# Later chunks copy x ahead of routing, and weight fetches move with seven raw buffers

## The chip, the cores and the metric

One core of a Trainium2 chip runs the kernel. The metric is device time in microseconds (us); lower is better. The engines are TensorE (PE in the rows, its weight loads PEld), VectorE (DVE), ScalarE (ACT), GpSimd (POOL) and SyncE (SP), which issues most DMAs. Each engine works through its own instructions in program order.

## The reference

Two stages follow each other: a linear attention with a decaying state (batch 4, 8 heads, 768 steps, head size 48), and a mixture of 8 experts with one expert per token (top 1) over its 3072 output rows.

```python
for t in range(S):
    cur = einsum('bhd,bhe->bhde', u[None] * k_t, v_t)
    y_t = einsum('bhd,bhde->bhe', r_t, state + cur)
    state = w[None, :, :, None] * state + einsum('bhd,bhe->bhde', k_t, v_t)
x = y.transpose(0, 2, 1, 3).reshape(3072, 384)
logits = x @ w_gate                      # 8 experts
expert = argmax(logits); gate = softmax(logits)[expert]
# each expert takes its tokens in order, up to a capacity of 768
out[i] = gate[i] * (relu(x[i] @ w1[expert]) @ w2[expert])
```

## The kernel before

**Attention.** The 3072 rows are worked on in NI = 24 chunks of 128, one turn of the loop `for i in range(NI)` each. PE makes score products (`scores`, L448), the value and state products (`values` L484, `inter` L493) and the state update (L459). DVE applies the mask (`masks`, L451) and copies the chunk's result out of PSUM (`turn`, L497, tile `yt`). In the next turn PE transposes that copy (`flip`, L504) and makes the router's logits from it (`logits`, L511). Two or three products without use (`fresh`, L524) stand ahead of `flip`. ACT copies the transposed rows (`rows`, L515) and SP stores them in the DRAM tensor `x_dr` (L519).

**Routing.** When the logits of a group of chunks are there, a generator `route` does that group in stages: `choose` on DVE (L76 to L111, ending with `lane`), rank products on PE (L114 to L117), slots and gate values on DVE (L121 to L158), a product on PE that turns them into table entries (L169), and the addition to the table on DVE (L171). `advance("t")` runs the next stage that waits for PE, `advance("v")` the next of DVE. The group of chunks 18 to 20 goes through `choose` in turn 21, its slots in turn 22 and its table product in turn 23. The group of chunks 21 to 23 comes after the loop. When chunks 0 to 17 are in the table, `ide` (L173) names the first 256 rows of expert 0 and POOL gathers them; `ids` (L175) names all the rest after the last group, and POOL then issues one gather per tile of rows (`gather`, L249, tile `xg`).

**After the loop.** PE transposes the 256 gathered rows (L263); ACT and DVE split them in two parts `xh` and `xl` (L267, L268), so that each fp32 product is made of three. The *early* part multiplies them with the first weights of expert 0 (`early`, L301 to L303, tile `e`), with the last stages of routing between its eight steps. Six products without use (`warm`, L547) follow, then PE transposes the two other tiles of expert 0 (L263) and makes their first layer (`layer1`, L280 to L282). From there PE runs layer 1 and layer 2 (L319 to L321) of the eight experts.

**Weights.** SP fetches raw weights into a pool `wrw` with `bufs=4` (`fetch`, L224, or in two halves L664 in the loop); ACT and DVE split each raw buffer into two parts `ws` (`split`, L234 and L235). A raw buffer is free for the next fetch when its two splits are done. `PLAN0` says in which turn a fetch or a split of expert 0 stands; `next(ws)` does its next entry. In turn 22 it splits entries 6 and 7, in turn 23 entry 8, entries 9 to 13 stand in the early part. `w1s` is the same for expert 1; it starts after the loop, with two of its three first fetches in the early part.

Of the kernel before, what the change touches and what calls it, by code (L numbers as in the profile page):

```python
# [19 lines left out]
NI = B * NC  # L20
# [6 lines left out]
PLAN = [((0, 1, 2), ())] + [((n // 2 + 3,) if n % 2 == 0 and n < 8 else (), (n,)) for n in range(14)]  # L27
# [7 lines left out]
def rwkv_moe(nc, tc, dmj, rkv, bdc, wp, wv, uv, wgp, wg, w1, w2, out, cap):  # L35
# [3 lines left out]
    with ExitStack() as ctx:  # L39
# [57 lines left out]
        def advance(slot, most=1 << 30):  # L97
            for r in list(routing):
                if r[1] == slot and most:
                    most -= 1  # L100
                    r[1] = next(r[0], None)
                    if r[1] is None:
                        routing.remove(r)
# [93 lines left out]

        with ExitStack() as mc:
            wsp = [mc.enter_context(tc.tile_pool(name="wsp", bufs=1))]
            wrw = mc.enter_context(tc.tile_pool(name="wrw", bufs=4))  # L200
            keep = mc.enter_context(tc.tile_pool(name="keep", bufs=1))
            sm = mc.enter_context(tc.tile_pool(name="sm", bufs=2))
            ps1 = mc.enter_context(tc.tile_pool(name="ps1", bufs=1, space=PSUM))
# [8 lines left out]
            def wset(e):  # L212
                wtiles[e] = [wsp[e % 2].tile([128, 3 if i < 2 else 8, F if i < 2 else DM], F32R,
                                             tag=f"ws{i}", name=f"ws{i}_{e}") for i in range(4)]
                return wtiles[e]

            def wstream(e, plan, later=None):
                raw = {}

                def fetch(k):  # L220
                    r = raw[k] = wrw.tile([128, F if k < 3 else 2 * DM], F32, tag="wr", name=f"wr{k}_{e}")
                    src = w1[e, :, k] if k < 3 else w2[e, :, 2 * k - 6:2 * k - 4].rearrange("p f d -> p (f d)")
                    if later is None:
                        nc.sync.dma_start(out=r, in_=src)  # L224
                    else:
                        later.extend([(r[64 * h:64 * h + 64], src[64 * h:64 * h + 64]) for h in range(2)])

                def split(n):
                    k, j = divmod(n, 2)
                    m, i, o = (0, k, 512) if k < 3 else (2, n - 6, DM)  # L230
                    c = slice(o * j, o * j + o) if k < 3 else slice(0, DM)
                    hi, lo = (wtiles[e][m + t][:, i, c] for t in range(2))
                    r = raw[k][:, o * j:o * j + o]
                    nc.scalar.copy(out=hi, in_=r)  # L234
                    nc.vector.tensor_tensor(out=lo, in0=r, in1=hi.bitcast(F32), op=ALU.subtract)  # L235

                for fetches, splits in plan:
                    if splits and e not in wtiles:
                        wset(e)
                    for k in fetches:  # L240
                        fetch(k)
                    for n in splits:
                        split(n)
                    yield
# [242 lines left out]
            def inter(i):  # L487
                t = T[i]
                if t["s0"] is None:
                    return  # L490
                for p in range(NP):
                    for a in range(2):
                        nc.tensor.matmul(yrows(p, a), lhsT=t["s0"][row(a), p], rhs=t["rt"][row(a), p], start=False, stop=p >= 2)  # L493

            def turn(i):
                yt = T[i]["yt"] = wk.tile([PR, 2, 256], F32, tag="yt", name=f"yt{i}")
                nc.vector.tensor_copy(out=yt, in_=py[0:PR, :, 0:256])  # L497
# [39 lines left out]
            def each(f, i, *more):  # L537
                if i < NI:
                    f(i, *more)
# [124 lines left out]
                    nc.sync.dma_start(out=r, in_=src)  # L664

            ws = wstream(0, PLAN0, parts)
            more = setup3()
            for i in range(NI):
                if i >= 2:
                    store(i - 2, nc.sync)  # L670
                part()
                each(product, i + 3)
                each(diag, i + 2, range(0, 2))
                each(scores, i + 1)
                if i == 0:
                    warm(2)
                else:
                    fresh(i - 1, 2)
                    flip(i - 1)
                    rows(i - 1)  # L680
                advance("t")
                each(update, i + 1)
                if i >= 1:
                    logits(i - 1)
                    if i + 3 >= NI:
                        keep_turn(i - 1)
                each(diag, i + 2, range(2, NP))
                if i == NI - 2:
                    gather(0, ide, (0, 1), C * SNAP)
                each(masks, i + 1)  # L690
                each(prep_k, i + 3)
                each(carry, i + 1)
                each(prep_state, i + 3)
                each(load, i + 7, 1)
                each(load, i + 7, 2)
                part()
                if i >= NI - 2:
                    next(ws)
                if i == NI - 1:
                    store(i - 1, nc.sync)  # L700
                advance("v")
                values(i)
                each(load, i + 6, 3)
                if i == 0:
                    bonus_alone(3)
                elif i + 3 < NI:
                    bonus(i + 3, lg[:, E:])
                if 0 < i < NI - 3:
                    keep_turn(i - 1)
                inter(i)  # L710
                turn(i)
                each(prep_r, i + 3)
                each(load, i + 7, 0)
                if i >= 1:
                    next(more, None)
                if i < NI - 2:
                    next(ws)
            while parts:
                part()
            w1s = wstream(1, [((k,), ()) for k in range(3)] + PLAN[1:])  # L720
            next(w1s)
            lc.close()
            buf = mc.enter_context(tc.tile_pool(name="act", bufs=1, side="right"))
            hh, hl = (buf.tile([128, 8, W1S], F32R, name=n) for n in ("hh", "hl"))
# [9 lines left out]
            keep_turn(NI - 1, lo)  # L734
            rows(NI - 1)
            store(NI - 1, nc.sync)
            for s_ in [xtrans(0, j, (0, 1)) for j in range(3)]:
                s_()
            advance("v")
            for f in range(8):  # L740
                if f % 2 == 0:
                    product_, split_ = early(f // 2)
                product_(f % 2)
                if f in (0, 2, 5):
                    advance("t")
                    advance("v")
                if f == 2:
                    gather(0, ids[:, 0:4], (2, 3))
                    gather_all(1)
                if f % 2:  # L750
                    split_()
                if f > 2:
                    next(ws, None)
                if f in (3, 5):
                    next(w1s)
            assert not routing
            warm(6)
            ac.close()
# [5 lines left out]
            ws = w1s  # L764
# [4 lines left out]
            for k in range(E):  # L769
# [10 lines left out]
                if k + 1 < E:  # L780
# [5 lines left out]
                    if k + 2 < E:  # L786
                        ws = wstream(k + 2, PLAN)
# [246 lines left out]
```

## Time and profile before

| what | value |
|---|---|
| median of 3 runs | 410.23 us (409.98 to 411.45) |
| profiled execution | 410.22 us |
| its span, first to last instruction | 408.4 us |
| PE busy | 386.5 us, 95% of the span |
| PEld busy | 349.0 us, 85% |
| DVE busy | 242.8 us, 59% |
| ACT busy | 190.1 us, 47% |
| POOL busy | 139.9 us, 34% |
| moved by DMA | 59.23 MB, 145 GB/s over the span |

The shares are means over stages with different limits, so the stage is looked at by itself. The chain that ended last is 58% PE, 21% issue, 8% DVE, 5% DMA and 5% POOL. About 1.8 us of the profiled execution lie outside its span.

### The profile page before, as it was taken

To read this page: it belongs to the slowest core of one execution; us is meant where nothing else is said; L and a number is where in the kernel's file an instruction comes from. 1 tells how busy PE (TensorE), PEld (TensorE's weight loads), DVE (VectorE), ACT (ScalarE), POOL (GpSimd) and SP (SyncE) were. 2 spreads that over 40 slices of the span, in tenths; PEclk is the share of its full clock that TensorE was granted. 3 is DMA by queue.
4 is the path that set the end of the run, shared out by engine and by line. 5 is a ranking of instruction groups with operands and counts; after the bars stand their busy time and mean duration, and the time that the engine had idled before them with its cause. 6 is when DMAs were issued, how large, how long until landed. Compare 5 with 4: busy or idle time off the path is not lost.

```text
span 408.4 us, 10083 instructions
## 1 busy us (share of the span) xinstructions
PE 386.5 (95%) x3883; PEld 349.0 (85%) x3884; DVE 242.8 (59%) x546; ACT 190.1 (47%) x496; POOL 139.9 (34%) x198
## 2 busy tenths in 40 slices
PE   8999999999999685999999999999999999999993
PEld 4588888888877574999999999999999999999992
DVE  6587989999998564654644635635635535534310
ACT  3666666676654132532733733633633633622401
POOL 3677468478443016103303303303303300300203
PEclk9999999999999698899999999999999999999998
DMA  6786997977723306354444444444544533500102
GB/s 175 230 245 196 262 241 237 241 236 206 215 81 87 102 20 211 107 155 157 146 134 158 135 134 156 136 139 146 148 134 152 155 126 91 161 16 1 58 1 69
DMA packets 28714, 59.23 MB, mean 145 GB/s; under 512 B 5194, under 2 KB 14450, under 8 KB 28656
## 3 DMA queue, kind: packets, MB, share of 16 engines
q1 hardware_dynamic: 25072, 49.05, 41.7%
q0 software_dynamic: 3584, 9.44, 6.9%
q8 instruction: 32, 0.52, 0.6%
q14 instruction: 26, 0.21, 0.2%
HBM read 49.38 MB, written 9.78 MB: 145 GB/s over the span
## 4 chain that ended last, share of the span: by engine, by line
PE 58%; issue 21%; DVE 8%; DMA 5%; POOL 5%; another core or an unknown queue 1%; SPq 1%; POOLq 1%; ACT 0%; DVEq 0%
PE b L319 6%; PE a L280 5%; PE a L281 5%; PE a L282 5%; PE b L320 5%; PE b L321 5%; POOL out L328 4%; PE pk L448 3%; PE warm L547 3%; DMA dm<-dmj 3%; PE py L484 2%; PE tp L263 2%; DMA wr<-w 2%; PE py L493 2%; PE pu L411 2%
## 5 line engine op out<-in xcount | busy, mean ns | idle before, releaser
L235 DVE TENSOR_TENSOR ws<-wr,ws 128x384 fp32r<-128x384 f32 (+1 forms) x112 | 66.7, 613 | 5.1 <-ACT ws L234 4.4
L328 POOL DMA_INDIRECT out<-yo,ids x32 | 31.2, 976 | 108.9 <-ACT yo L327 102.1
L280 PE MATMUL a<-xh,ws 128*128 128x412 f32 (+1 forms) x192 | 68.3, 356 | 0.0
L319 PE MATMUL b<-hh,ws 128*128 128x412 f32 (+1 forms) x192 | 68.0, 354 | 0.0
L282 PE MATMUL a<-xh,ws 128*128 128x412 f32 (+1 forms) x192 | 66.0, 343 | 0.0
L281 PE MATMUL a<-xl,ws 128*128 128x412 f32 (+1 forms) x192 | 65.9, 343 | 0.0
L320 PE MATMUL b<-hl,ws 128*128 128x412 f32 (+1 forms) x192 | 65.7, 342 | 0.0
L321 PE MATMUL b<-hh,ws 128*128 128x412 f32 (+1 forms) x192 | 65.7, 342 | 0.0
L249 POOL DMA_INDIRECT xg<-x_dr,ids x30 | 30.2, 1006 | 101.8 <-PE tp L263 74.7
L285 ACT ACTIVATE hh<-a 128x412 fp32r<-128x412 f32 (+1 forms) x64 | 31.2, 488 | 71.9 <-PE a L282 71.9
L286 DVE SCALAR_TENSOR_TENSOR hl<-a,hh 128x412 fp32r<-128x412 f32 (+1 forms) x64 | 35.4, 553 | 45.2 <-ACT hh L285 43.4
L234 ACT CAST ws<-wr 128x384 fp32r<-128x384 f32 (+1 forms) x112 | 59.9, 557 | 0.0
L322 DVE COPY yt<-b 128x412 f32<-128x412 f32 (+1 forms) x24 | 13.7, 570 | 72.6 <-PE b L321 56.7
L424 ACT ACTIVATE s<-idn,lb 128x128 f32<-128x128 f32 x160 | 51.1, 392 | 0.5
L404 POOL TENSOR_TENSOR z<-dm 112x256 f32<-112x256 f32 x48 | 38.1, 813 | 7.4 <-DMA dm<-dmj 7.4
L267 ACT CAST xh<-tp 128x412 fp32r<-128x412 f32 (+2 forms) x27 | 12.4, 469 | 54.8 <-PE tp L263 52.9
L280 PEld LDWEIGHTS a<-xh,ws 128*128 128x128 f32 x192 | 36.8, 192 | 0.2
L319 PEld LDWEIGHTS b<-hh,ws 128*128 128x128 f32 x192 | 36.1, 188 | 0.9
L281 PEld LDWEIGHTS a<-xl,ws 128*128 128x128 f32 x192 | 36.8, 192 | 0.1
L282 PEld LDWEIGHTS a<-xh,ws 128*128 128x128 f32 x192 | 36.6, 191 | 0.1
L320 PEld LDWEIGHTS b<-hl,ws 128*128 128x128 f32 x192 | 36.2, 188 | 0.1
L321 PEld LDWEIGHTS b<-hh,ws 128*128 128x128 f32 x192 | 36.1, 188 | 0.2
(161 smaller groups left out, 624.2 us busy)
## 6 DMA issues: line engine op xcount, KB each, us to landing
wr<-w SPq DMA_DIRECT2D x21, 512.0 KB
wr<-w SPq DMA_DIRECT2D x28, 384.0 KB
dm<-dmj SPq DMA_DIRECT2D x88, 96.0 KB
bk<-bdc SPq DMA_DIRECT2D x24, 192.0 KB
bv<-bdc SPq DMA_DIRECT2D x24, 192.0 KB
x_dr<-x SPq DMA_DIRECT2D x24, 192.0 KB
wr<-w SPq DMA_DIRECT2D x6, 256.0 KB
wr<-w SPq DMA_DIRECT2D x8, 192.0 KB
```

Of the source, the lines that this page charges most:

```text
L234: nc.scalar.copy(out=hi, in_=r)
L235: nc.vector.tensor_tensor(out=lo, in0=r, in1=hi.bitcast(F32), op=ALU.subtract)
L280: nc.tensor.matmul(o, lhsT=wh, rhs=xh[:, d, a:z], start=d == 0, stop=False)
L281: nc.tensor.matmul(o, lhsT=wh, rhs=xl[:, d, a:z], start=False, stop=False)
L282: nc.tensor.matmul(o, lhsT=wl, rhs=xh[:, d, a:z], start=False, stop=d == 2)
L286: nc.vector.scalar_tensor_tensor(out=hl[:, f, b:z], in0=o[:, b - a:], scalar=0.0, in1=hh[:, f, b:z].bitcast(F32), op0=ALU.max, op1=ALU.sub ...
L319: nc.tensor.matmul(o, lhsT=wh, rhs=hh[:, f, :n], start=f == 0, stop=False)
L320: nc.tensor.matmul(o, lhsT=wh, rhs=hl[:, f, :n], start=False, stop=False)
L321: nc.tensor.matmul(o, lhsT=wl, rhs=hh[:, f, :n], start=False, stop=f == 7)
L328: r = nc.gpsimd.indirect_dma_start(out=out[:, :], out_offset=bass.IndirectOffsetOnAxis(ap=ids[:q, at:at + 1], axis=0), in_=yo, in_offset=N ...
L404: nc.gpsimd.tensor_tensor(out=z[:, p:p + 2], in0=t["dm"][:, 0, p:p + 2], in1=t["dm"][:, 1, p:p + 2], op=ALU.mult)
L424: nc.scalar.mul(out=s[:, a, p], in_=idn, mul=t["bon"][:, 2 * p + a:2 * p + a + 1])
```

## The change

In turns 21 to 23 `advance("t")` goes from ahead of `update` to behind `inter`, and `advance("v")` from ahead of `values` to behind `turn`. `next(ws)` is the last step of every turn now. The fetch plan of expert 1 is made ahead of the loop, and one of its three w1 fetches (512 KB) is issued at the end of each of turns 21, 22 and 23; the two fetches in the early part are gone. The pool `wrw` has 7 buffers. After the loop, `choose` of the last group stands ahead of the splits of the early rows, and the split of the first early tile is issued in step 2, behind the routing stage there, and not in step 1.

```diff
-            wrw = mc.enter_context(tc.tile_pool(name="wrw", bufs=4))
+            wrw = mc.enter_context(tc.tile_pool(name="wrw", bufs=7))
...
             ws = wstream(0, PLAN0, parts)
+            w1s = wstream(1, [((k,), ()) for k in range(3)] + PLAN[1:])
...
-                advance("t")
+                if i < NI - 3:
+                    advance("t")
                 each(update, i + 1)
...
                 part()
-                if i >= NI - 2:
-                    next(ws)
                 if i == NI - 1:
                     store(i - 1, nc.sync)
-                advance("v")
+                if i < NI - 3:
+                    advance("v")
                 values(i)
...
                 inter(i)
+                if i >= NI - 3:
+                    advance("t")
                 turn(i)
+                if i >= NI - 3:
+                    advance("v")
+                    next(w1s)
                 each(prep_r, i + 3)
                 each(load, i + 7, 0)
                 if i >= 1:
                     next(more, None)
-                if i < NI - 2:
-                    next(ws)
+                next(ws)
             while parts:
                 part()
-            w1s = wstream(1, [((k,), ()) for k in range(3)] + PLAN[1:])
-            next(w1s)
...
-            for s_ in [xtrans(0, j, (0, 1)) for j in range(3)]:
+            flipped = [xtrans(0, j, (0, 1)) for j in range(3)]
+            advance("v")
+            for s_ in flipped:
                 s_()
-            advance("v")
...
-                if f % 2:
+                if f == 2:
+                    early_()
+                if f == 1:
+                    early_ = split_
+                elif f % 2:
                     split_()
                 if f > 2:
                     next(ws, None)
-                if f in (3, 5):
-                    next(w1s)
```

The first place is DVE in turns 22 and 23. Before, `masks` (L451) is followed by two weight splits (L235), the slots and values of the routing group (L121 to L158), and only then the copy of chunk 22 (L497, `yt_2585`):

```order
L451 COPY_PREDICATED s_2426<-msk,pk 128x1024
L235 TENSOR_TENSOR ws_0_1137<-wr_0_1839,ws_0_1136 128x384 x2
L121 TENSOR_TENSOR pr<-pr,oh_2483 128x24
...
L158 TENSOR_TENSOR at_2564<-pr,lo_2555 128x384
L497 COPY yt_2585<-py 112x512
L235 TENSOR_TENSOR ws_0_1137<-wr_0_2120,ws_0_1136 128x384
L171 TENSOR_TENSOR tab<-tab,pr 128x96
L497 COPY yt_2629<-py 112x512
```

In the change, on the same engine at the same place (the copies of chunks 22 and 23 are `yt_2567` and `yt_2630`):

```order
L451 COPY_PREDICATED s_2426<-msk,pk 128x1024
L497 COPY yt_2567<-py 112x512
L121 TENSOR_TENSOR pr<-pr,oh_2501 128x24
...
L158 TENSOR_TENSOR at_2580<-pr,lo_2571 128x384
L235 TENSOR_TENSOR ws_0_1137<-wr_0_1839,ws_0_1136 128x384 x2
L497 COPY yt_2630<-py 112x512
L171 TENSOR_TENSOR tab<-tab,pr 128x96
L235 TENSOR_TENSOR ws_0_1137<-wr_0_2120,ws_0_1136 128x384
```

The copy of chunk 22 moved ahead of the routing and of the two splits; the copy of chunk 23 stands behind both. In turn 21 the copy likewise moved ahead of the table addition and `choose`, which stand ahead of L451 in both kernels.

The second place is DVE after the loop, where `xl` is the split of the early rows, `lane` the end of `choose` and `hl` the split of an early tile. Before:

```order
L268 TENSOR_TENSOR xl<-tp_2_0_2679,xh 128x256
L76 TENSOR_REDUCE pr<-lb 128x3
...
L111 TENSOR_TENSOR lane<-lane,pr 128x8
L121 TENSOR_TENSOR pr<-pr,oh_2693 128x24
...
L158 TENSOR_TENSOR at_2720<-pr,lo_2716 128x384
L308 SCALAR_TENSOR_TENSOR hl<-e_2699,hh 128x2x256
L171 TENSOR_TENSOR tab<-tab,t_2747 128x32
L175 TENSOR_SCALAR ids<-tab 128x32
```

In the change:

```order
L76 TENSOR_REDUCE pr<-lb 128x3
...
L111 TENSOR_TENSOR lane<-lane,pr 128x8
L268 TENSOR_TENSOR xl<-tp_0_0_2677,xh 128x256
...
L121 TENSOR_TENSOR pr<-pr,oh_2691 128x24
...
L158 TENSOR_TENSOR at_2724<-pr,lo_2720 128x384
L171 TENSOR_TENSOR tab<-tab,t_2749 128x32
L175 TENSOR_SCALAR ids<-tab 128x32
```

`choose` moved ahead of the three splits, and the first `hl` went behind `ids` and the gate values.

The third place is SP's queue from turn 21 to the first fetches of w2 (`wr_0` are buffers of expert 0, `wr_1` of expert 1; 128x1024 is a w1 fetch of 512 KB, 128x768 a w2 fetch of 384 KB). Before:

```order
L519 DMA x_dr<-x_2340 128x384
L519 DMA x_dr<-x_2446 128x384
L664 DMA wr_0_2507<-w 64x768 x2
L519 DMA x_dr<-x_2525 128x384
L519 DMA x_dr<-x_2595 128x384
L224 DMA wr_1_2631<-w 128x1024
L519 DMA x_dr<-x_2670 128x384
L224 DMA wr_1_2790<-w 128x1024
L224 DMA wr_1_2822<-w 128x1024
L224 DMA wr_1_2906<-w 128x768
```

In the change:

```order
L519 DMA x_dr<-x_2340 128x384
L224 DMA wr_1_2507<-w 128x1024
L519 DMA x_dr<-x_2446 128x384
L664 DMA wr_0_2509<-w 64x768 x2
L224 DMA wr_1_2585<-w 128x1024
L519 DMA x_dr<-x_2527 128x384
L519 DMA x_dr<-x_2599 128x384
L224 DMA wr_1_2633<-w 128x1024
L519 DMA x_dr<-x_2674 128x384
L224 DMA wr_1_2906<-w 128x768
```

The three w1 fetches stand among the stores of chunks 19 to 23, and the first w2 fetch comes directly behind the last store. The buffers that the second and third w1 fetch of before waited for (those of entries 9 and 11) are taken by the second and third w2 fetch in the change.

## Rows read from the trace of the kernel before

**Rows 1.** The page's 40 slices of the span (10.2 us each), in tenths, and GB/s.

```profile
PE   8999999999999685999999999999999999999993
PEclk9999999999999698899999999999999999999998
...
GB/s 175 230 245 196 262 241 237 241 236 206 215 81 87 102 20 211 107 155 157 146 134 158 135 134 156 136 139 146 148 134 152 155 126 91 161 16 1 58 1 69
```

**Rows 2.** Windows: start:end length, busy us per engine, granted clock, DMA share, GB/s.

```profile
165.00:401.00 236.00, 236.00 (x1353) 228.01 (x1352) 112.95 (x217) 100.50 (x214) 50.91 (x52) 1.00 0.39 118
```

**Rows 3.** PE's timeline, turn 21 to early part: start, us, what, [idle <-releaser].

```profile
125.91 0.40 PE L169 MATMUL pr<-val,at 128*128 128x96 f32 x2
126.24 0.56 PE L459 MATMUL pu<-bv,kt 128*48 128x48 f32 x16
...
128.08 0.66 PE L493 MATMUL py<-rt,st 48*48 48x128 f32 x16
...
130.65 0.60 PE L504 MATMUL xp<-idn,yt 112*128 112x112 f32 x4 [0.28 <-DVE yt L497]
...
132.75 0.65 PE L493 MATMUL py<-rt,st 48*48 48x128 f32 x16
...
137.18 1.01 PE L504 MATMUL xp<-idn,yt 112*128 112x112 f32 x4 [3.24 <-DVE yt L497]
...
143.61 0.64 PE L511 MATMUL lo<-wgt,yt 112*64 112x8 f32 x16
...
148.22 0.17 PE L114 MATMUL pr<-oh,tri 128*128 128x24 bf16 x1 [1.04 <-DVE lane L111]
```

**Rows 4.** DVE's timeline over the same stretch.

```profile
127.83 0.24 DVE L171 TENSOR_TENSOR tab<-tab,pr 128x96 f32<-128x96 f32 x1
...
129.91 0.68 DVE L497 COPY yt<-py 112x512 f32<-112x512 f32 x1
130.51 1.29 DVE L451 COPY_PREDICATED s<-msk,pk 128x1024 f32<-128x1024 int32 x1
132.62 1.03 DVE L235 TENSOR_TENSOR ws<-wr,ws 128x384 fp32r<-128x384 f32 x2 [0.81 <-ACT ws L234]
133.56 0.18 DVE L121 TENSOR_TENSOR pr<-pr,oh 128x24 f32<-128x24 f32 x1
...
135.98 0.55 DVE L158 TENSOR_TENSOR at<-pr,lo 128x384 fp32r<-128x384 int32 x1
...
145.61 1.08 DVE L268 TENSOR_TENSOR xl<-tp,xh 128x256 fp32r<-128x256 f32 x3 [2.35 <-ACT xh L267]
```

**Rows 5.** Windows with the granted clock (the number ahead of the DMA share).

```profile
137.20:143.40 6.20, 6.20 (x58) 4.67 (x58) 1.41 (x3) 1.05 (x3) 0.00 (x0) 0.50 0.36 119
164.00:167.00 3.00, 3.00 (x14) 2.72 (x15) 0.64 (x2) 0.72 (x3) 1.95 (x2) 0.50 0.41 144
167.30:172.00 4.70, 4.70 (x42) 4.70 (x41) 3.92 (x9) 3.46 (x9) 0.00 (x0) 1.00 0.24 64
```

**Rows 6.** PE's timeline from the end of the early part.

```profile
156.52 1.47 PE L547 MATMUL warm<-wz 128*128 128x512 bf16 x6
157.83 0.44 PE L263 MATMUL tp<-idn,xg 128*128 128x128 f32 x2
163.18 1.35 PE L263 MATMUL tp<-idn,xg 128*128 128x128 f32 x4 [4.91 <-remote]
```

**Rows 7.** Waits between 150 and 165 us: us in total, times, longest.

```profile
ACT hh L307 <- remote: 4.5, 1, 4.5
```

**Rows 8.** Windows of 2 us around that wait.

```profile
156.00:158.00 2.00, 2.00 (x13) 1.12 (x12) 1.20 (x3) 0.00 (x0) 1.70 (x2) 1.00 0.91 318
158.00:160.00 2.00, 0.27 (x2) 0.13 (x1) 0.00 (x0) 0.00 (x0) 1.39 (x3) 1.00 0.96 352
```

**Rows 9.** First gather by `ids` (POOL's timeline), three weight fetches (SP's, 150 to 165).

```profile
151.65 1.00 POOL L249 DMA_INDIRECT xg<-x_dr,ids  x1 [20.03 <-DVE pr L91]
...
153.94 8.51 SPq L224 DMA_DIRECT2D wr<-w  x3
```

## The prediction

> **What bounds the kernel now.** I read the page's slices first, to find where the end is decided. PE is full except in slices 14 to 16, which span 133 to 163 us, and the clock dips in the same place [rows 1]. From 165 to 401 us PE is busy in all 236 us at full clock [rows 2]: the experts start when the stage before lets them, and nothing behind it can absorb or return a gain. So the question is by how much the first layer of expert 0 starts earlier. Weight buffers and prefetch in the expert stage are hidden by PE itself.
>
> I then followed PE through that stage, asking of each idle time who ended it. In turn 23 PE waits 3.24 us for DVE's copy of chunk 22 [rows 3]. DVE had the chunk's result at 133.4, when `inter` (132.75, 0.65 long) ended, but had two weight splits and the slots of a routing group in its queue until 136.53 [rows 3, 4]. [...] A second idle time of 1.04 us comes at 148.22, where the rank product waits for `lane`, the end of `choose` [rows 3]. The third is the longest: after `warm` and two transposes PE stops for 4.91 us until 163.18, with no releaser that the profile knows [rows 6], and ACT waits 4.5 us in the same way for a tile whose products PE had long made [rows 7]. It falls in the only place where DMA moves 318 to 352 GB/s over 4 us, against a mean of 20 in the slice before [rows 1, 8]. After it the clock is at 0.50 once more until about 167.3 [rows 5].
>
> **The change, step by step.**
>
> *Turn 21.* The table product (two matmuls, 0.33 us from 125.91 to the next row at 126.24) goes behind `inter`, which ends at 128.4 in place of 128.74 [rows 3]. DVE copies chunk 21 at once (0.68 us, to 129.1), then does table addition and `choose` (127.83 to 129.91 before, 2.08 us) until 131.2 and `masks` (1.29 us) until 132.5 [rows 4]. `masks` ended at 131.8 before, so 0.7 us later; nothing asks for its result until `values` of turn 23. PE's wait of 0.28 us ahead of `flip` in turn 22 is gone [rows 3].
>
> *Turn 22.* `inter` ended at 133.40. It loses that 0.28 us and about 0.2 us of rank products that go behind it: 132.95. DVE is free at 132.5, copies chunk 22 until 133.65, and `flip` runs at 133.7 in place of 137.18. **That is 3.5 us.**
>
> *Turn 23.* From `flip` to the end of `inter` PE took 2.75 us in turn 22 at full clock (130.65 to 133.40) [rows 3], 2.55 without the rank products: 136.3. But DVE still has the slots and values (133.56 to 136.53, 2.97 us) and the two splits (1.03 us) ahead of the copy of chunk 23 [rows 4]: 133.65 + 2.97 + 1.03 = 137.65, and the copy ends at 138.3. DVE, not PE, decides here. `lo` starts at 138.4 and not at 143.61: **5.2 us in all**, the 3.5 us included. What is left of idle PE time is under 1 us in two pieces; 1.04 us did not bring the clock down at 148.22, so I leave it up. [...]
>
> *Early part.* `choose` takes 1.53 us (from the end of `xl` at 146.69 to the rank at 148.22) [rows 3, 4]. It moves into the time in which DVE waits 2.35 us for ACT's `xh` [rows 4], but starts only with the last logits, so about 0.5 us of it pushes `xl`. The 1.04 us wait becomes about 0.35 us ahead of the third product: **0.7 us**, between 0 and 1.04. The first `hl` behind `ids` costs nothing: layer 2 needs it only when all of layer 1 is done, and it lets `ids` and the gathers come 0.7 us earlier too, so the gathers keep their lead on PE.
>
> So far 5.2 + 0.7 = 5.9 us: 410.2 - 5.9 = 404.3 us. This rests on waits of engines for each other and is the firm part.
>
> *The stop at 158 us.* Here the trace gives a coincidence and no cause. Before, two w1 fetches of 512 KB are issued from 153.94 on, as splits free two buffers, on top of the gathers that began at 151.65 [rows 9]. In the change those w1 fetches are done by then. But the same two buffers are now wanted by w2 fetches, which SP holds ready, so the same two releases start 384 KB each. The burst gets thinner, 768 KB for 1024, and does not disappear. The first of its fetches also comes later against the gathers, since one `hl` (about 0.7 us) is now ahead of the split that frees the buffer. Bounds: nothing of the 4.91 us is left, or all of it. Before, 4.05 us lie from the first fetch (153.94) to the end of `warm` (157.99) [rows 6, 9]; now about 3.4. Scaling by bytes and by that time, 4.91 x 0.75 x 3.4 / 4.05 = 3.1 us are left, an estimate between the two ends; 1.8 us are won.
>
> *The clock behind it.* [...] It fell behind idle times of 3.24 and 4.91 us and not behind 1.04. With 3.1 us it could go either way; I let it stay up, since part of the old fall came in a stop half as long again: 2.05 us won. Sum: 5.9 + 1.8 + 2.05 = 9.75 us, so **400.5 us**, by the profiled execution's own 410.22, which is the median of the runs but for 0.01. The 1.8 us outside the span stay.
>
> *The rest.* Three more buffers, and the fetches moved up: SP issues them among the stores of chunks 19 to 23, and only the gathers by `ids` wait for the last of these stores. DMA moves 81 to 102 GB/s in the slices from 112 to 143 us, where the first eleven slices reach 262 [rows 1], so 512 KB per turn fits. Nothing, then, as long as that store lands before `ids` is there; each us beyond would delay the late gathers by as much.
>
> **The rivals.**
>
> *The stop goes wholly* (A): no burst is dense enough to hold PE. 4.91 + 2.05 more than the firm part: 397.3 us. For it: nowhere else in the trace does PE stop so, in slices of up to 262 GB/s [rows 1]. Against: the same two releases.
>
> *The stop stays whole* (C): 404.3 us. For it: its length isn't explained by bytes, since it lasted until 163.18, after the densest window [rows 8]. [...]
>
> *The stop moves up* (D), the case on the other side: in turn 22 one w1 fetch and 384 KB of expert 0 now meet the two gathers by `ide`. If PE's hand-over to a copy is held there as at 158 us, 4.9 + 2.05 us are added to 404.3: 411.3 us, slower than before. It decides from a hold of 5.9 us on. For it: the densest windows were reached with two fetches and gathers in flight [rows 8, 9], and here two fetches and two gathers meet. Against: gathers and a 384 KB fetch ran there before without it.
>
> *The copy stays behind DVE* (E): turn 23 gains only the 3.5 us, or the clock falls in it, and the stop is whole: 406 to 408 us.
>
> **How the numbers follow.** A 0.27, my forecast 0.37 (with the clock down it is 402.5), C 0.22, D 0.07, E 0.07. The range from 396.8 to 404.9 holds the first three and leaves out D, E and a little. About 0.5% (2 us) is what a measurement can tell here from no change. Faster by more: 0.91 (A, forecast, C, most of E). Within: 0.05. Slower: 0.04.
>
> **What would show it.** `flip` of turn 23 about 3.5 us after the one of turn 22 began and at full clock; L235 twice directly ahead of the copy of chunk 23; `lo` at 138 to 139; no wait ahead of L114; the first L280 near 153 if A holds, 156 if I am right, 158 to 160 if C. It is wrong if PE's clock is at 0.50 anywhere from 133 to 150, if the transposes of the late tiles wait for a gather by name, or if layer 1 of expert 0 has gaps, in which case w2 and w1 of the next experts have moved the burst under it.

## The result, and the profile after

The changed kernel takes 405.81 us (median of 4 runs, 404.90 to 406.39) beside 410.11 for the kernel before: a ratio of 0.9887, 95% interval [0.9858, 0.9916]. The gain is 4.3 us. The forecast was 9.7. Every ratio in this document is of fast runs alone, those within 1.5% of the fastest of their kernel. The profiled execution of the changed kernel takes 405.67 us with a span of 403.9.

The slices of its page (10.1 us each, in tenths, and GB/s), which answer to [rows 1]:

```profile
PE   8899999999989894999999999999999999999993
...
PEclk9999999999999997999999999999999999999999
...
GB/s 178 232 237 218 259 239 226 253 209 223 235 69 138 189 123 153 140 110 145 210 78 144 207 80 142 208 80 137 216 80 141 217 82 79 60 2 1 59 1 69
```

The hole of before in slices 14 and 15 is all but closed (8 and 9 now). One hole is left, slice 16 with its 4, and the clock dips in the same slice. PE's timeline from turn 22 to the early part, answering to [rows 3]:

```profile
130.12 0.55 PE L504 MATMUL xp<-idn,yt 112*128 112x112 f32 x4
...
133.79 0.60 PE L504 MATMUL xp<-idn,yt 112*128 112x112 f32 x4 [0.36 <-DVE yt L497]
...
136.74 0.54 PE L169 MATMUL pr<-val,at 128*128 128x96 f32 x3 [0.28 <-DVE at L158]
...
138.37 0.64 PE L511 MATMUL lo<-wgt,yt 112*64 112x8 f32 x16 [0.43 <-DVE yt L497]
...
141.25 0.39 PE L303 MATMUL e<-xl,ws 128*128 128x256 f32 x1 [0.37 <-DVE xl L268]
...
142.17 0.19 PE L114 MATMUL pr<-oh,tri 128*128 128x24 bf16 x1
```

`flip` of turn 23 waits 0.36 us where it waited 3.24, `lo` starts at 138.37 where it started at 143.61, and the rank product (L114) waits for nothing. DVE's timeline shows why, answering to [rows 4]: the copies (L497) come as soon as PE has the chunk, and only the copy of chunk 23 stands behind splits.

```profile
133.04 0.69 DVE L497 COPY yt<-py 112x512 f32<-112x512 f32 x1 [0.92 <-PE py L493]
133.65 0.18 DVE L121 TENSOR_TENSOR pr<-pr,oh 128x24 f32<-128x24 f32 x1
...
136.60 1.01 DVE L235 TENSOR_TENSOR ws<-wr,ws 128x384 fp32r<-128x384 f32 x2
137.54 0.68 DVE L497 COPY yt<-py 112x512 f32<-112x512 f32 x1
```

The stop is still there. PE's timeline behind the early part, answering to [rows 6], and then ACT's line among the waits from 145 to 165 us, answering to [rows 7]:

```profile
150.72 1.24 PE L547 MATMUL warm<-wz 128*128 128x512 bf16 x5
151.79 0.44 PE L263 MATMUL tp<-idn,xg 128*128 128x128 f32 x2
157.28 1.35 PE L263 MATMUL tp<-idn,xg 128*128 128x128 f32 x4 [5.04 <-remote]
```

```profile
ACT hh L307 <- remote: 7.3, 1, 7.3
```

And the windows around it, answering to [rows 5, 8] (granted clock, DMA share and GB/s are the last three numbers):

```profile
150.00:152.00 2.00, 1.93 (x13) 1.10 (x12) 1.92 (x5) 0.00 (x0) 1.54 (x2) 1.00 0.83 294
152.00:154.00 2.00, 0.24 (x2) 0.13 (x1) 0.00 (x0) 0.00 (x0) 1.53 (x2) 1.00 0.71 181
154.00:156.00 2.00, 0.00 (x0) 0.00 (x0) 0.00 (x0) 0.00 (x0) 1.44 (x2) 1.00 0.67 230
...
157.20:163.40 6.20, 6.01 (x24) 5.16 (x25) 2.85 (x7) 2.60 (x8) 2.12 (x2) 0.50 0.32 92
163.40:163.80 0.40, 0.40 (x6) 0.40 (x5) 0.19 (x1) 0.40 (x2) 0.00 (x0) 1.00 0.00 0
```

PE went on at 163.18 before and goes on at 157.28 now: 5.90 us earlier, as the forecast's firm part has it. That it agrees to the hundredth is partly luck: the first two transposes come 6.04 us earlier (157.83 and 151.79), and the stop, 0.13 us longer, takes that surplus back. Then some of the gain is lost again. Before, PE worked 4.1 us at a granted clock of 0.50 behind the stop (163.2 to 167.3, [rows 5, 6]); now it is 6.1 us (157.3 to 163.4). The clock itself is no longer down than before: it stands at 0.50 from 160.4 to 167.2 before and from 156.5 to 163.3 now. But before, the first 2.8 us of that fell into the stop, when PE had nothing to do, and now only 0.8 us, as a window of before and then one of the change show:

```profile
160.00:162.00 2.00, 0.00 (x0) 0.00 (x0) 1.06 (x2) 1.00 (x2) 1.66 (x2) 0.60 0.36 104
```

```profile
156.00:156.40 0.40, 0.00 (x0) 0.00 (x0) 0.00 (x0) 0.00 (x0) 0.00 (x0) 1.00 0.10 38
```

Two more us at a clock of 0.50 in place of 1.00 cost 1.0 us, an estimate from these stretches, and PE has 0.2 us of gaps in that stretch (6.01 busy of 6.20). 5.90 - 1.0 - 0.2 = 4.7, and the two profiled executions differ by 410.22 - 405.67 = 4.55.

### The profile page after: what moved, and what is told of

Its sections match the earlier page's. It is cut to its first block, busy times and chain, and to the rows that moved or that the text cites. A ratio compares the mean times of both kernels' runs of the same rounds, so it can differ in the third digit from the quotient of the medians.

```text
span 403.9 us, 10057 instructions
## 1 busy us (share of the span) xinstructions
PE 382.8 (95%) x3856; PEld 347.8 (86%) x3884; DVE 241.9 (60%) x546; ACT 189.7 (47%) x496; POOL 139.7 (35%) x198
## 4 chain that ended last, share of the span: by engine, by line
PE 53%; issue 22%; DVE 11%; POOL 5%; DMA 5%; another core or an unknown queue 2%; SPq 1%; ACT 1%; POOLq 1%; DVEq 0%; ACTq 0%
PE b L319 6%; PE a L281 5%; PE a L282 5%; PE a L280 5%; PE b L320 5%; PE b L321 5%; POOL out L328 4%; PE warm L547 3%; DVE s L451 3%; PE pk L448 3%; PE py L484 2%; DMA bk<-bdc 2%; PE tp L263 2%; PE py L493 2%
## 5 line engine op out<-in xcount | busy, mean ns | idle before, releaser
L235 DVE TENSOR_TENSOR ws<-wr,ws 128x384 fp32r<-128x384 f32 (+1 forms) x112 | 66.7, 613 | 1.2 <-ACT ws L234 0.5
```

## The experiments

Four theories of the stop come up below. **W**: the weight fetches beside it hold PE. **G**: the run of eight indirect gathers holds it (PE went on 2.2 us after the last of them began in the kernel before, 2.5 in the changed one). **H**: the hand-over is late whatever is under way. **S**: it belongs to the conditions of the run and not to the program. The runs are in five series. The first two are from chip 0, the next three from chips 14, 15 and 4; the chip of the first pair is not known. Each series has its own runs of the kernel before, and their time is given with it.

### First series: gathers, fetches, the order alone, another tile for warm

`e1_late1`: the gathers of expert 1 behind the late tiles' transposes.

```diff
                     gather(0, ids[:, 0:4], (2, 3))
-                    gather_all(1)
...
                 xtrans(0, j, (2, 3))()
+            gather_all(1)
             gather_all(2)
```

> From the changed kernel, the four gathers of expert 1 are issued behind the transposes of expert 0's late tiles, not behind the two gathers of those tiles; all the weight fetches stay. Theory G (PE's hand-overs are held while a run of eight gathers is worked off: in both kernels PE went on 2.2 to 2.5 us after the last of the eight began): two gathers are through near 150.5 us, the stop of 5.04 us at 152 is gone or under 1 us, and with it the half clock behind it: 397 to 399 us. If the four gathers hold PE where they stand now, the stop comes in layer 1 of expert 0 and 403 to 405 are left. Theory W (the weight fetches in the stop hold PE): the stop and the time stay, 405 to 406.

`e2_hold`: SP waits for the last `xh` of expert 0 ahead of the w2 fetches of expert 1.

```diff
+        hold = dram.tile([1, W1S - EARLY], F32, name="hold")
         idn = const.tile([128, 128], F32, name="idn")
...
                 xtrans(0, j, (2, 3))()
+            nc.sync.dma_start(out=hold, in_=xh[0:1, 2, EARLY:W1S].bitcast(F32))
             gather_all(2)
```

> From the changed kernel, a transfer of 624 bytes on SP that waits for the last xh of expert 0 stands ahead of the w2 fetches of expert 1, so no weight fetch is under way from about 146 us to the end of the stop; the gathers stay as they are. Theory W: the stop of 5.04 us shrinks to under 1 us, 398 to 400 us. Theory G: the stop stays between 4.5 and 5.1 us, 405 to 407 us (a little more if the late fetches keep a split of expert 1 waiting).

`e3_order`: the new order alone.

```diff
-            wrw = mc.enter_context(tc.tile_pool(name="wrw", bufs=7))
+            wrw = mc.enter_context(tc.tile_pool(name="wrw", bufs=4))
...
-                    next(w1s)
...
+            w1s = wstream(1, [((k,), ()) for k in range(3)] + PLAN[1:])
+            next(w1s)
             lc.close()
...
+                if f in (3, 5):
+                    next(w1s)
             assert not routing
```

> The changed order of turns 21 to 23 and of choose and the first hl, but four raw weight buffers and the three w1 fetches of expert 1 where they were before. By the forecast's firm part the order alone gives all of it, so the stop (near 5 us) and the time are those of the changed kernel: 405 to 406.5 us. If the buffers and the early fetches matter (rival: they thin the burst that the stop comes from), the stop is longer or the time over 407.

`e4_warmtag`: the last `warm` writes the tile of tag rk (the seventh call of `warm` is the one ahead of the late tiles).

```diff
-                t = ps1.tile([128, 512], F32, tag="xp", name=f"warm{len(heat)}")
+                t = ps1.tile([128, 512], F32, tag="xp" if len(heat) < 7 else "rk", name=f"warm{len(heat)}")
```

> From the changed kernel, the six warm products ahead of the late tiles write the PSUM tile of tag rk, so that the second transpose of a late tile no longer waits for them. If only this hand-over of PE to itself were late, the stop would be gone and the time 398 to 400 us. If PE's signals to all engines are held (theory G and W alike), ACT still waits near 7 us for the early rows' last product, the second transposes come near 152 us, and layer 1 starts no earlier than before: 405 to 406.

The kernel before took 403.17 us in this series, 7 us less than in the first pair, and the four took 397.32, 397.21, 397.20 and 397.54. None has a stop. What the edits have in common is only that they ran here, so none of them can be credited. In `e3_order`, with the program's gathers and the old fetches, the windows of the old stop are as dense as any of before, and PE is busy throughout:

```profile
150.00:152.00 2.00, 2.00 (x11) 1.00 (x9) 1.35 (x3) 1.27 (x4) 1.64 (x2) 1.00 0.92 292
152.00:154.00 2.00, 2.00 (x17) 1.90 (x16) 0.83 (x4) 0.88 (x4) 1.53 (x2) 1.00 1.00 376
```

### Second series: both kernels again, and the two parts alone

`r_after` and `r_before` are the two kernels without an edit.

> The changed kernel, unaltered, once more. Four edited versions of it ran near 397.3 us beside a kernel before at 403.2, and all without the stop. Theory S (the stop belongs to the conditions of the first pair of runs and to no part of either program): it has none here either, the tiles of the late rows follow without a gap over 1 us, 397 to 398 us. Rival P (each of the four edits happened to take the stop away): the stop of 5 us is back and with it the half clock, 405 to 406.

> The kernel before, unaltered, for its profile. Theory S: no stop near 158 us, 4.91 us and some 2 us of half clock behind it are gone, 403 us; the waits of turn 23 (3.24 us) and ahead of the rank product (1.04 us) stand as in the first profile. Rival P: the stop is there, and the 403 has another reason.

The kernel before takes 402.80 us (16 runs), the changed one 397.21: ratio 0.987 [0.9848, 0.9892], 5.6 us between the medians. PE's timeline at the place of the stop, first of the kernel before, then of the changed one:

```profile
155.98 1.47 PE L547 MATMUL warm<-wz 128*128 128x512 bf16 x6
157.28 1.30 PE L263 MATMUL tp<-idn,xg 128*128 128x128 f32 x6
158.51 0.38 PE L280 MATMUL a<-xh,ws 128*128 128x256 f32 x1
```

```profile
150.07 1.47 PE L547 MATMUL warm<-wz 128*128 128x512 bf16 x6
151.38 1.30 PE L263 MATMUL tp<-idn,xg 128*128 128x128 f32 x6
152.61 0.38 PE L280 MATMUL a<-xh,ws 128*128 128x256 f32 x1
```

All six transposes stand in one row without a wait, and the first products of layer 1 take 0.38 us, not the 0.58 that they took at a clock of 0.50 in the first pair. The program is the same as in the first pair, so theory S holds: the stop is not made by this program alone. From 157.28 to 151.38 it is 5.90 us again, and here they reach the end: the spans differ by 401.2 - 395.3 = 5.9.

`p_choose`: on the kernel before, `choose` and the first `hl` only.

```diff
-            for s_ in [xtrans(0, j, (0, 1)) for j in range(3)]:
+            flipped = [xtrans(0, j, (0, 1)) for j in range(3)]
+            advance("v")
+            for s_ in flipped:
                 s_()
-            advance("v")
...
-                if f % 2:
+                if f == 2:
+                    early_()
+                if f == 1:
+                    early_ = split_
+                elif f % 2:
                     split_()
```

> One part alone, on the kernel before: choose ahead of the three splits of the early rows, and the first hl behind ids. The forecast's term is 0.7 us (between 0 and 1.04): the wait ahead of the rank product is under 0.4 us, 0.2 to 0.3% faster. Rival: what choose delays (xl and the third product) costs as much, and nothing is won.

`p_turns`: on the kernel before, turns 21 to 23 only.

```diff
-                advance("t")
+                if i < NI - 3:
+                    advance("t")
...
-                if i >= NI - 2:
-                    next(ws)
...
-                advance("v")
+                if i < NI - 3:
+                    advance("v")
                 values(i)
...
                 inter(i)
+                if i >= NI - 3:
+                    advance("t")
                 turn(i)
+                if i >= NI - 3:
+                    advance("v")
...
-                if i < NI - 2:
-                    next(ws)
+                next(ws)
```

> The other part alone, on the kernel before: in turns 21 to 23 the copy of x ahead of routing and of the weight splits; four raw buffers, the fetches where they were, choose where it was. The forecast's term is 5.2 us (3.5 if the clock falls all the same, 6.5 if PE decides): about 1.3% faster, lo near 138.4 us. Rival: without the early fetches and the three buffers some of it is lost to a later wait, under 0.8% is left.

`p_turns` takes 398.00 us, ratio 0.988 [0.9861, 0.9899]: 4.8 us of the 5.2 forecast. `lo` starts at 138.10 where the kernel before has it at 143.07 in this series, and the wait ahead of the rank product is untouched. PE's timeline of `p_turns`:

```profile
138.10 0.64 PE L511 MATMUL lo<-wgt,yt 112*64 112x8 f32 x16 [0.43 <-DVE yt L497]
...
142.71 0.17 PE L114 MATMUL pr<-oh,tri 128*128 128x24 bf16 x1 [1.05 <-DVE lane L111]
```

`p_choose` takes 402.46, ratio 0.9985 [0.9968, 1.0002]: 0.6 us by the ratio, with an interval that includes no gain at all. The trace is clearer than the times: the wait of 1.04 us ahead of L114 is gone, and the third product waits instead:

```profile
146.46 0.39 PE L303 MATMUL e<-xl,ws 128*128 128x256 f32 x1 [0.38 <-DVE xl L268]
```

That is 0.66 us of waiting less, as forecast (0.7). The buffers and early fetches give nothing: `e3_order` (397.20) without them is `r_after` (397.21) with them, both on chip 0.

### Third series: the clock in turn 23, and the order in more turns

`c_warm23`: the kernel before with 14 more dummy products in the wait of turn 23.

```diff
-                    fresh(i - 1, 2)
+                    fresh(i - 1, 16 if i == NI - 1 else 2)
```

> The kernel before, with 14 more dummy products (512 columns, 0.21 us each at full clock, some 3 us) ahead of flip in turn 23, in PE's wait of 3.2 us for the copy of chunk 22. Nothing else moves, so the wait for the copy stays; only PE's clock can change. If the clock is a part of the 4.8 us that the turns won, the granted clock stays at 1.00 from 130 to 150 us, lo comes some 2 to 3 us earlier and the time falls by as much, near 400.3 us. If only the waits matter, or the clock falls all the same, 402.8.

`v_order5` and `v_order8`: the changed kernel with the new order from turn 19 and from turn 16 on.

```diff
-                if i < NI - 3:
+                if i < NI - 5:
                     advance("t")
...
-                if i >= NI - 3:
+                if i >= NI - 5:
                     advance("t")
                 turn(i)
-                if i >= NI - 3:
+                if i >= NI - 5:
                     advance("v")
+                if i >= NI - 3:
                     next(w1s)
```

> From the changed kernel, the new order (copy of x ahead of routing) also in turns 19 and 20. In the changed kernel flip of turns 20 and 21 still wait 0.61 and 0.60 us for the copies of chunks 19 and 20, which stand behind routing on DVE. If DVE has room behind them, both waits are gone: 396.0 to 396.6 us where the changed kernel has 397.2. Rival: DVE has no idle time from 103 to 127 us, so what is put off makes the masks or a later copy late by as much: no gain.

> The same from turn 16 on. There the copies are not waited for, so it should be like the version from turn 19 on (within 0.3 us); if putting routing off gathers on DVE until it delays masks, it is slower than that.

`r_after2` is the changed kernel without an edit.

> The changed kernel, unaltered, beside the two versions above: 397.2 us without the stop, as in the run before. If the stop of the first pair is there in this series, it shows in the kernel before too (410 instead of 403 us), and its length says whether it follows the order of DVE's work.

In this series, on chip 14, the kernel before takes 410.46 us and the stop is back in all four: 4.96 us in `c_warm23`, 5.00 in `v_order5`, 5.02 in `v_order8`, 4.96 in `r_after2`. The changed kernel takes 405.68, ratio 0.9879 [0.985, 0.9907]. So the stop comes with the chip or the time of the runs and not with the version, and where it comes its length does not depend on the order of DVE's work or on how much earlier PE arrives.

`c_warm23` takes 408.80, ratio 0.9958 [0.9936, 0.998]: 1.7 us. Its `flip` still starts at 137.43, but the granted clock is 1.00 where [rows 5] have 0.50, and `lo` comes at 141.28, 2.3 us earlier than in [rows 3]. Two rows of PE's timeline and two windows of it:

```profile
137.43 0.60 PE L504 MATMUL xp<-idn,yt 112*128 112x112 f32 x4 [0.53 <-DVE yt L497]
141.28 0.64 PE L511 MATMUL lo<-wgt,yt 112*64 112x8 f32 x16 [0.15 <-DVE yt L497]
```

```profile
137.00:140.00 3.00, 2.57 (x51) 2.33 (x55) 0.83 (x2) 1.05 (x3) 0.00 (x0) 1.00 0.20 69
140.00:143.00 3.00, 2.80 (x44) 1.93 (x35) 0.95 (x3) 0.67 (x3) 0.00 (x0) 1.00 0.63 177
```

So of the 5.2 us by which the turns bring `lo` forward, some 2.3 are the clock, with the wait left as it is, and 2.9 the rest. Dummy products alone, with no other change, were worth a third of the whole in this series (1.7 of 4.8 us). Behind the stop a part of the 2.3 is lost again: PE goes on behind it at 160.89, 2.29 us earlier than in [rows 6], but then works 6.2 us at a clock of 0.50 (to 167.1) where the kernel before worked 4.1.

`v_order5` has a ratio of 0.999 [0.9951, 1.0028] to the kernel before (all its runs: 407.60 to 417.78 us), where the changed kernel has 0.9879 in the same series: the whole gain is lost, which is worse than its rival's "no gain". `v_order8` has too few runs for a ratio (410.08 to 422.81 us; its profiled execution takes 414.94). Two rows of PE's timeline of `v_order5` show the new waits:

```profile
121.22 1.08 PE L484 MATMUL py<-s,bv 128*48 128x128 f32 x16 [1.41 <-DVE rt L429]
...
123.37 0.63 PE L411 MATMUL pu<-uz,z 112*64 112x2 f32 x16 [1.06 <-DVE q L473]
```

`rt` is `prep_r` of chunk i + 3, which DVE does behind `turn`; routing now stands between the two. Turns 21 to 23 have no `prep_r` left to do. That makes the new order free of these waits there, and not two turns earlier. By the rows, the waits are the smaller part of the loss, though. In `r_after2` `flip` waits 0.82 and 0.80 us in turns 20 and 21 and not in `v_order5`, so PE waits only 0.85 us more, and the two profiled executions are 2.65 us apart (408.17 and 405.52). The rest is mainly the clock, as PEclk of the pages shows, first of `r_after2`, then of `v_order5` and `v_order8`:

```profile
PEclk9999999999999997899999999999999999999997
PEclk9999999999998998799999999999999999999997
PEclk9999999999895999699999999999999999999998
```

Behind the new waits the clock of `v_order5` is at 0.50 from 125.8 to 129.2 us, that of `v_order8` from 108.7 to 112.1 and from 122.4 to 136.0; that of `r_after2` stays at 1.00 up to the stop. Half clock for 3.4 us costs about 1.7 us, for 17 us about 8.5, an estimate from these stretches.

### Fourth and fifth series: what the stop is tied to

The fourth series met the stop, on chip 15 (the kernel before at 409.37). `s_late`, `s_hold` and `s_tag` are the kernels `e1_late1`, `e2_hold` and `e4_warmtag` again; `s_both` has the edits of the first two.

> The version with the gathers of expert 1 behind the late tiles' transposes, again, for a chip on which the stop occurs (the kernel before at 410). Theory G (the run of gathers): two gathers stand ahead of the stop in place of six, PE goes on 2.2 to 2.5 us after the start of the second of them or does not stop at all, 397 to 400 us. Theory W (weight fetches) and theory H (the hand-over itself, whatever is under way beside it): the stop stays at 4.9 to 5.1 us, 405 to 406. On a chip without the stop: 397.3 beside 403, and nothing is told.

> The version with no weight fetch under way during the stop, again. Theory W: the stop shrinks to under 1 us, 398 to 400. Theories G and H: 4.9 to 5.1 us of stop, 405 to 406. Without the stop on this chip: 397.2 beside 403.

> The version with warm in the tile of tag rk, again. If PE's wait for its own products alone is late, the stop is gone. If PE's signals to all engines are late (theories G, W and H), the second transposes come at once, but ACT waits for the early rows' last product as before, and layer 1 starts no earlier: 405 to 406. Without the stop on this chip: 397.5 beside 403.

> The gathers of expert 1 late and the weight fetches held, both: only two gathers are under way at the stop. Theories G and W, alone or together: no stop, 397 to 400 us. Theory H: 4.9 to 5.1 us of stop all the same, 405 to 406. Without the stop on this chip: 397 to 398 beside 403.

They take 404.43, 404.91, 403.30 (one run) and 403.97 us. PE's rows behind the stop, in the order `s_late`, `s_hold`, `s_tag`, `s_both` (in `s_hold` and `s_both` a line is added ahead, so their L264 is L263):

```profile
157.32 1.35 PE L263 MATMUL tp<-idn,xg 128*128 128x128 f32 x4 [4.89 <-remote]
```

```profile
156.13 1.35 PE L264 MATMUL tp<-idn,xg 128*128 128x128 f32 x4 [4.12 <-remote]
```

```profile
150.95 1.30 PE L263 MATMUL tp<-idn,xg 128*128 128x128 f32 x6
156.66 0.58 PE L280 MATMUL a<-xh,ws 128*128 128x256 f32 x1 [4.40 <-ACT xh L267]
```

```profile
155.08 1.35 PE L264 MATMUL tp<-idn,xg 128*128 128x128 f32 x4 [3.41 <-remote]
```

`s_late` was a bad test. Nothing that POOL waits for stood ahead of the moved gathers, and POOL began the first of expert 1 at 148.38 and went on without a gap, as in the changed kernel (148.19). `s_hold` is a good one. The fetches are out of the stop, as the windows of `s_late` (first) and `s_hold` from 150 to 155 us show, 253 against 89 GB/s:

```profile
150.00:155.00 5.00, 2.44 (x16) 1.42 (x14) 1.35 (x3) 0.00 (x0) 3.90 (x4) 1.00 0.74 253
```

```profile
150.00:155.00 5.00, 2.01 (x12) 1.00 (x10) 1.34 (x3) 1.00 (x2) 3.78 (x5) 1.00 0.30 89
```

The stop goes from 4.89 to 4.12, and to 3.41 in `s_both`, whose gathers run as in `s_hold`; so these two differ by 0.7 us without a cause in the program that I can name, and theory W explains 0.8 to 1.5 us of the stop at most. Even that bought no time that the runs can tell. `s_tag` shows that it is not PE's wait for itself: with that dependence gone all six transposes run at once, and the stop is now ACT's, which still gets the word that the early rows' last product is done only at 154.79, so that layer 1 waits for `xh`. PE's signals are late for ACT (5.83 us of waiting, with no releaser that the profile knows) as well as for PE. No theory has its number here: with the fetches held, W asked for a stop under 1 us, and G and H for 4.9 to 5.1.

For theory G two kernels made POOL really wait.

```diff
                 xtrans(0, j, (2, 3))()
+            scrap = keep.tile([1, 4], F32, name="scrap")
+            nc.gpsimd.tensor_copy(out=scrap, in_=xh[0:1, 2, W1S - 4:W1S].bitcast(F32))
+            gather_all(1)
             gather_all(2)
```

That is `g1_pool` (without the `gather_all(1)` of the early part); `g2_poolsp` holds SP as `e2_hold` does as well.

> From the changed kernel, a copy of four words on POOL that reads the last xh of expert 0 stands ahead of the gathers of expert 1, so only the two gathers of expert 0's late tiles are under way in the stop (through by some 150 us); the weight fetches stay. Theory G: stop under 1 us, 397 to 400 us (the gathers of expert 1 still come some 10 us before they are wanted, if they do not make a new stop in layer 1). Theory H (the hand-over as such, whatever is under way): 4.9 to 5.1 us of stop, 404 to 406. Without the stop on this chip: 397 to 398 beside 403.

> The same, with the weight fetches held as in s_hold as well: from about 150 us to the end of the stop DMA has next to nothing to do. Theory G, with or without a share of the fetches: no stop, 397 to 400 us. Theory H: 3.4 us or more of stop, as in s_hold and s_both, 403 to 405. Without the stop on this chip: 397 to 398 beside 403.

This series ran on chip 4, without the stop (the kernel before at 403.34): 396.97 us for `g1_pool`, ratio 0.9844 [0.9827, 0.986], and 399.51 for `g2_poolsp`, 0.9922 [0.9897, 0.9947]. Of what makes the stop it tells nothing. It does tell that the gathers of expert 1 can begin 5 us later (153.72) at no cost, and that with the fetches held as well they come too late, since PE's next row waits for them in `g2_poolsp`:

```profile
162.93 0.50 PE L264 MATMUL tp<-idn,xg 128*128 128x128 f32 x2 [1.39 <-DMA xg<-x_dr,ids]
```

`g1_pool` stands at the best ratio of all, but its interval overlaps that of the changed kernel (0.987 on another chip), and they were not run side by side: I don't count it as a faster version.

## Why the prediction was wrong, step by step

*Turns 21 to 23: right.* `flip` of turn 23 at 133.79 (forecast 133.7), the two L235 directly ahead of the copy of chunk 23, `lo` at 138.37 (138.4), clock at 1.00 from 130 to 156, where before it was 0.50 behind the wait of 3.24 us (137.2 to 143.4, [rows 5]). By itself the part measures 4.8 us (forecast 5.2, interval about 4 to 5.6). The lower bound of 3.5 us that `p_turns` names, for a clock that falls all the same, was not tested: `c_warm23` keeps the wait and takes away the low clock, and that is worth 2.3 us.

*Early part: right.* 1.04 us of waiting became 0.37; `p_choose` alone 0.6 us with an interval that includes no gain.

*Buffers and fetches: right.* They cost nothing and give nothing.

The firm sum of 5.9 us is what both pairs of profiles show at the last transposes, 5.90 and 5.90, in the first pair with 0.13 us of a longer stop in it.

*The stop at 158 us: the step that failed.* The forecast had "a coincidence and no cause", and scaled its 4.91 us by bytes and by time to 3.1, 1.8 us won. It stayed at 5.04, 0.13 us lost, although the windows in it were thinner (294, 181 and 230 GB/s) than those of before. The wait is one that the program does not make alone: both kernels ran with it in the first pair and without it on chip 0; chips 14 and 15 had it in every profile, chips 0 and 4 in none. Rival C, "the stop stays whole", was the case that happened, at 404.3 forecast and 405.81 measured. Its argument, a length that bytes do not explain, agrees with the stop of 5.04 us under the thinner burst; the 0.8 to 1.5 us that held fetches took off in single profiles neither bear it out nor settle it, and where the stop comes from is not shown.

*The clock behind it: the second failure, and it follows from the first.* I let the clock stay up (2.05 us won, half of the 4.1 us that PE worked at 0.50 behind the old stop in [rows 5, 6], an estimate), since the stop was to be shorter. No run shows these 2.05 us by themselves; what the pair showed in their place is a clock that fell to 0.50 again, and for 6.1 us of work and not 4.1, since it fell later in the stop. So the term is -1.0 and not +2.05. With the stop whole, the sum by the measured terms is 410.22 - 5.90 + 1.0 + 0.2 = 405.5, against 405.67.

The number of rival A, 397.3 us, is what the changed kernel takes on a chip without the stop (397.21), but not for A's reason: there the kernel before is at 402.80 too, and the gain is again that of the firm part. The case on the other side (D) did not occur: the clock and `flip` of turn 22 show no hold.

What stays open: what in the chip makes the stop, and whether the gathers have a part in it. PE went on 2.2 to 2.5 us after the start of the eighth gather in seven profiles, but 1.4 and 0.7 us after it in `s_hold` and `s_both`, so that tie is loose; the two kernels that hold the gathers back did not meet a chip with the stop. One more thing was not tried: every run here was taken with the records of a profile, so none shows whether the stop is there without them.

The traces have something on it, all the same: in none of them does the stop come without a loss of records. The ten profiles with a stop hold 5892 to 6059 records of semaphore updates (the signals by which engines and DMA queues release each other), the ten without 6414 to 6428. Up to 110 us they agree (3256 in the kernel before with the stop, 3264 without); nearly all that is missing lies behind 145 us (2349 for 2793), most of it landings of DMA. The list of DMA issues shows it for the gathers by `ids`, in the kernel before with the stop (no time to landing can be given) and in `r_before`, the same program without:

```profile
xg<-x_dr,ids POOLq DMA_INDIRECT x30
```

```profile
xg<-x_dr,ids POOLq DMA_INDIRECT x30, 3.4
```

Whether the loss has a part in the stop, or something else makes both, is not shown.

## What to carry to other kernels

A wait with no releaser that the profile knows is not a term to be scaled: price it once as unchanged and once as gone, and before building on it look whether it is there on another chip. Work that an idle engine waits for goes ahead of work that nobody waits for, but count what stands behind it on the same engine: the same order was worth 4.8 us in the turns with no `prep_r`, and taken two turns further up it lost the whole gain, by new waits (1.41 and 1.06 us) and by the clock of 0.50 behind them. And when an idle time lets the clock fall, ask what the clock alone is worth: 14 more dummy products, with the clock at 1.00 and not 0.50 behind the wait, gave a third of the gain of the turns (1.7 of 4.8 us).

## What the runs showed of the hardware

- A stop of one length at one place in the program, on some chips: 4.89 to 5.04 us in seven profiles with the gathers and fetches not held back (chips 14, 15 and that of the first pair), none in ten profiles on chips 0 and 4. The kernel before takes about 410 us with it and 403 without.
- Where the stop is, some 350 to 540 of about 6420 records of semaphore updates are missing from the profile, nearly all of them from the stretch behind 145 us.
- Around it the waits for PE's signals have no releaser that the profile knows: ACT 7.29, PE itself 5.04, DVE 1.17 us in the changed kernel.
- The length of an idle time alone does not tell for how long PE then works at a granted clock of 0.50: 4.1 us behind a stop of 4.91, 6.1 us behind one of 5.04, since before the clock had fallen 2.8 us ahead of PE's next work, and now 0.8 us.
- DMA at a share of 1.00 and 376 GB/s beside a PE that is busy all the time, in `e3_order`.
